# Relative-bias attention and a mixture of adapters: the bias row laid out anew, and the start-up order rewritten

## The chip, the cores and the metric

One core of a Trainium2 chip runs the whole kernel. The core has a matrix engine (PE in the profile; its weight loads are PEld), a vector engine (DVE), a scalar engine for activations (ACT), a general-purpose vector engine (GpSimd, POOL in the profile) and SyncE (SP), which here only issues transfers. Transfers are also issued from ACT and from POOL; all run on the core's 16 DMA engines. The metric is the device time of one execution, in microseconds (us).

## The reference

Eight batches of attention, eight heads, 576 positions, 64 values a head, with a bias that depends on the distance of two positions alone (at most 32 buckets, the last for every distance from 128 on); after it, on the rows of all heads side by side, a mixture of eight rank-16 adapters with the two best taken.

```python
B, H, S, D = 8, 8, 576, 64
scores = scale * q @ k.T                        # scale = 1/8
scores = scores + bias_table[bucket].transpose(2, 0, 1)[None]   # bucket = f(|i - j|)
attn = exp(scores - max) / sum
attn_out = attn @ v
x = attn_out as [B*S, H*D]                      # 4608 x 512
logits = x @ w_gate                             # 512 x 8, the two largest are kept, softmax of the two
out = x + sum over the two e of w_e * (x @ A[e]) @ B[e]
```

## The kernel before

**Tiling.** The 576 positions of a batch are 512 and a tail of 64. The 512 are dealt to partitions so that position 4p + j is partition p of group j, and the keys are cut into groups g = 0 to 3 of 128. Two heads, hp and hp + 4, make a pair; a batch has four pairs, and 32 pairs run through the kernel. Each pair has five steps: for g = 0 to 3 the scores of 128 keys against 512 queries for both heads, and for g = 4 the tails of both heads (tail keys against all queries, and all keys against the tail queries). That makes 160 steps. A step is `qk` on PE into one of two score buffers in PSUM (lines 375 and 381), `expo` on ACT (line 396), which turns 128 x 1024 scores into the probabilities p, and, for g below 4, `band_of` on DVE, which multiplies p near the diagonal with a table M of exp(bias).

**The bias.** Since the last bucket holds from distance 128 on, it is subtracted from all, and what is left is zero outside a band. For each head a row of 512 values over the signed distance is built in SBUF (`gg`: the row itself and its exponential, eight heads in eight partitions), written to DRAM (`g_d`), and read back so that each partition holds the stretch of the row that its own position needs: `Mr` (128 x 8 x 384, the exponentials, for M), `MHr` and `Br` (the plain row for the tails). From these, `band_table(hp)` on DVE copies M for one pair (line 287, 768 elements with the direction reversed), and `tail_bias(n)` on POOL copies B4 (n = 0 from MHr, n = 2 from Br) and BT (n = 1 from MHr). A tail step needs both parts of B4: PE adds them to the scores with a product by the identity (line 381, `sc<-B,ident`). BT goes into the 64 x 64 corner, `tail_scores` (lines 355 to 360).

**Other work of a pair.** `cast_kq` casts its k and q from f32 to bf16 (DVE for the first three pairs, POOL afterwards; `pkq` in the start-up list), `transposes` turns them on PE (line 337) with one copy on DVE (`kqT`), `cast_v` casts v, `pv` multiplies probabilities and values on PE (line 426, five slices: 0 to 3 for the 512 queries, 4 for the tail queries), `recip` and `norm` divide on DVE (`rn` in the list). Per batch: `tail_transposes` (line 346, `tt` in the list), `tail_scores` (`ts`), and the mixture of an earlier batch, spread over the steps by `MIX`: logits, gate in four parts, `m_z` (line 563), `m_zT`, four output blocks, tail output.

**Order.** Nothing is scheduled automatically: each engine runs its instructions in the order in which they are recorded. A step n records `qk(n+1)`, `expo(n)`, loads, the entries of `OPS[n]`, and then the regular work. `START` changes the order of the first 15 steps: the groups 0 to 3 of pairs 0, 1 and 2 come first, and then their tail steps, `(0, 4), (1, 4), (2, 4)`, as steps 12, 13 and 14. Step 15 is the first of pair 3, step 20 the first of batch 1. `OPS` holds the start-up work of steps 0 to 18: `ckq` casts of pairs 1 and 2, `T` transposes, `M` band tables, `b` bands, `cv` casts of v, `pv` and `rn`. `SPQ`, `POOLQ` and `POOLQ2` are the first transfers of SP and POOL, in order (`kq` k and q of a pair, `v` v of batch 0 in four parts of four transfers, `tl` and `vt` tails, `M`, `MH`, `Br` the three reads of the row). A cast on POOL made with `behind_dve` waits for the DVE instruction recorded just before it. The tail transfers of batch 1 are issued on POOL at steps 12 and 13.

The lines to follow: 71 (table load), 210 to 236 (the row), 238 (its write), 249, 257 and 263 (its three reads), 287 (M), 292, 296, 298 (tails), 175 (tail loads), 185 (casts on POOL), 305 (zeroing of second buffers on POOL). DVE's instructions all carry line 126, a helper that remembers the last one.

Of the kernel before, what the change touches and what calls it, by code (L numbers as in the profile page):

```python
# [10 lines left out]
FP32 = mybir.dt.float32  # L11
BF16 = mybir.dt.bfloat16
# [15 lines left out]
def kernel(  # L28
# [40 lines left out]
    btT = cp.tile([H, NB], FP32, tag="btT")  # L69
    for e in range(2):  # L70
        (nc.gpsimd if e else nc.scalar).dma_start(
            out=btT.rearrange("(c e) b -> e c b", e=2)[e],
            in_=bias_table.rearrange("b (e c) -> e c b", e=2)[e])
    warm = cp.tile([128, 1], FP32, tag="warm")
    nc.vector.memset(warm, 0.0)
    fill = cp.tile([128, 512], BF16, tag="fill")
    nc.vector.memset(fill, 1.0)
# [4 lines left out]
    START = ((0, 0), (0, 1), (0, 2), (0, 3), (1, 0), (1, 1), (1, 2), (1, 3), (2, 0), (2, 1),  # L82
             (2, 2), (2, 3), (0, 4), (1, 4), (2, 4))
    SPQ = (('v', 0), ('v', 1), ('M', 0, 8), ('v', 2), ('v', 3), ('kq', 0, 3), ('kq', 1, 0),
           ('kq', 1, 1), ('kq', 1, 2), ('kq', 1, 3), ('v1', 0), ('v1', 1), ('v1', 2),
           ('v1', 3))
    POOLQ = (('tl', 0, 0), ('tl', 0, 1), ('tl', 1, 0), ('tl', 1, 1), ('MH', 0), ('MH', 1),
             ('Br', 0), ('Br', 1), ('Br', 2), ('Br', 3))
    POOLQ2 = (('vt', 0), ('vt', 1), ('B', 0), ('B', 1), ('B', 2))
    OPS = {0: (('ckq', 1), ('T', 1)),  # L90
           3: (('ckq', 2),),
           4: (('T', 2),),
           5: (('pkq', 3, 0),),
           6: (('tt', 0),),
           7: (('pkq', 3, 1),),
           8: (('M', 0),),
           9: (('b', 0, 0), ('b', 0, 1)),
           10: (('M', 1), ('b', 0, 2), ('b', 0, 3), ('ts', 0), ('pkq', 4, 0)),
           11: (('cv', 0), ('b', 1, 0), ('b', 1, 1)),
           12: (('M', 2), ('b', 1, 2), ('b', 1, 3), ('T', 3), ('pkq', 4, 1)),  # L100
           13: (('cv', 1), ('b', 2, 0), ('b', 2, 1), ('pv', 0, 0), ('pv', 0, 1), ('pv', 0, 2),
                ('rn', 0, 0)),
           14: (('b', 2, 2), ('b', 2, 3), ('pv', 0, 3), ('pv', 0, 4), ('rn', 0, 1)),
           15: (('cv', 2), ('M', 3), ('pv', 1, 0), ('pv', 1, 1), ('pv', 1, 2), ('rn', 1, 0)),
           16: (('pv', 1, 3), ('pv', 1, 4), ('rn', 1, 1)),
           17: (('pv', 2, 0), ('pv', 2, 1), ('pv', 2, 2), ('rn', 2, 0)),
           18: (('cv', 3), ('tt', 1), ('pv', 2, 3), ('pv', 2, 4), ('rn', 2, 1))}
    LAST = ((2, 'pv', 0), (2, 'pv', 1), (1, 'eh', 7), (1, 'pv', 2), (1, 'pv', 3))

    def keep_busy(n, cols=512):  # L110
        ps = acp.tile([128, 512], FP32, name="fl", tag="acc")
        for _ in range(n):
            nc.tensor.matmul(ps[:, :cols], lhsT=fill[:, 0:128], rhs=fill[:, :cols],
                             start=True, stop=True, skip_group_check=True)
# [85 lines left out]
    for t in tls[:1] + vts[:1]:  # L200
# [7 lines left out]
    gg = cp.tile([H, 2, 512], BF16, tag="gg")  # L208
    g_sb = gg[:, 0]
    nc.gpsimd.memset(g_sb, 0.0)  # L210
    bsub = cp.tile([H, NB], FP32, tag="bsub")
    nc.gpsimd.tensor_scalar(bsub, btT, btT[:, NB - 1:NB], 1.0 / scale,
                      op0=ALU.subtract, op1=ALU.mult)
# [9 lines left out]
    while runs[nsm][0] == nsm and runs[nsm][2] == nsm + 1:  # L223
        nsm += 1
    nc.gpsimd.tensor_copy(g_sb[:, C:C + nsm], bsub[:, :nsm])
    nc.gpsimd.tensor_copy(
        g_sb[:, C - nsm + 1:C],
        bass.AP(tensor=bsub.tensor, offset=bsub.offset + nsm - 1,
                ap=[bsub.ap[0], [-1, nsm - 1]]))
    for bv, lo, hi in runs[nsm:]:  # L230
        n = hi - lo
        dst = bass.AP(tensor=g_sb.tensor, offset=g_sb.offset + C - hi + 1,
                      ap=[g_sb.ap[0], [hi - 1 + lo, 2], [1, n]])
        (nc.scalar.copy if bv % 3 else nc.gpsimd.tensor_copy)(
            dst, bsub[:, bv:bv + 1].unsqueeze(2).to_broadcast((H, 2, n)))
    nc.scalar.activation(gg[:, 1], g_sb, ACT.Exp, scale=scale)
    g_d = nc.dram_tensor("g_d", (H, 2, 512), BF16, kind="Internal")
    nc.scalar.dma_start(out=g_d.ap(), in_=gg)
# [4 lines left out]
    Mr = cp.tile([128, H, MW], BF16, tag="Mr")  # L243
    MHr = cp.tile([128, HP, 192], BF16, tag="MHr")
    Br = cp.tile([128, H, 64], BF16, tag="Br")

    def load_bias(h0, h1):
        for j in range(4):
            nc.sync.dma_start(
                out=Mr[j * 32:(j + 1) * 32, h0:h1],  # L250
                in_=bass.AP(tensor=gt.tensor, offset=gt.offset + h0 * 1024 + 512 + j,
                            ap=[[4, 32], [1024, h1 - h0], [1, MW]]))
# [3 lines left out]
    def load_br(j, eng):  # L256
        eng.dma_start(
            out=Br[j * 32:(j + 1) * 32],
            in_=bass.AP(tensor=gt.tensor, offset=gt.offset + 64 + j,
                        ap=[[4, 32], [1024, H], [1, 64]]))  # L260

    def load_mh(e, eng):
        eng.dma_start(
            out=MHr[e * 64:(e + 1) * 64],
            in_=bass.AP(tensor=gt.tensor, offset=gt.offset + e * 1024 + 192,
                        ap=[[1, 64], [2048, HP], [1, 192]]))

    for f, *a in SPQ:
        {"v": lambda j: load_v(0, (j,)), "M": load_bias, "kq": load_kq,
         "v1": lambda j: load_v(1, (j,)), "Br": lambda j: load_br(j, nc.sync),  # L270
         "MH": lambda e: load_mh(e, nc.sync)}[f](*a)
    for f, *a in POOLQ:
        {"tl": lambda w, e: load_tail(0, w, e), "Br": lambda j: load_br(j, nc.gpsimd),
         "MH": lambda e: load_mh(e, nc.gpsimd)}[f](*a)
# [7 lines left out]
    def at(t, off, *dims):  # L282
        return bass.AP(tensor=t.tensor, offset=t.offset + off,
                       ap=[t.ap[0]] + [list(d) for d in dims])

    def band_table(hp):
        dve.tensor_copy(M[:, 2 * hp:2 * hp + 2],
                        at(Mr, 2 * hp * MW + MW - 1, (MW, 2), (-1, 4), (-4, 96)))

    def tail_bias(n):  # L290
        if n == 0:
            return nc.gpsimd.tensor_copy(
                B4[:, :, 0:128].rearrange("p c (j u) -> p c j u", j=4),
                at(MHr, 191, (192, HP), (-1, 4), (-4, 32)))
        if n == 1:
            return nc.gpsimd.tensor_copy(BT.rearrange("p c (e t) -> p c e t", e=2),
                                         at(MHr, 63, (192, HP), (0, 2), (-1, 64)))
        nc.gpsimd.tensor_copy(  # L298
            B4[:, :, 128:256].rearrange("p c (e t) -> p c e t", e=2),
            at(Br, 63, (128, HP), (64, 2), (-1, 64)))  # L300

    for f, *a in POOLQ2:
        {"vt": lambda e: load_tail(0, 2, e), "B": tail_bias, "cv": cast_v}[f](*a)
    for t in tls[1:] + vts[1:]:
        nc.gpsimd.memset(t, 0.0)
    v_ones(nc.gpsimd, vts[1])
    nc.gpsimd.memset(vns[1][:, :, :, D:D1], 1.0)
# [522 lines left out]
    def pool_kq(i, w):  # L830
# [5 lines left out]
        "w": keep_busy, "vt": load_tail, "B": tail_bias,  # L836
        "ckq": lambda i: (cast_kq(i, 0, dve), cast_kq(i, 1, dve)), "pkq": pool_kq}

    MIX = (4, 9, 17, 19, 19, 19, 20, 20, 22, 24, 25, 27, 30, 32, 39)
# [110 lines left out]
```

## Time and profile before

| | us |
|---|---|
| three runs | 203.14, 203.54, 206.69 |
| median | 203.54 |
| the profiled execution, its own time | 202.09 |
| its span from the first to the last record | 200.3 |

In the profile a group of instructions is one line: where it starts, how long it was busy, engine, line of the kernel, what it writes and reads, how many, and in brackets how long the engine had been idle before it and what released it. Steps can be counted off on ACT: every `p<-sc` is one step, the first at 7.58 us. Counted so, step 11 starts at 18.97 us, step 14 at 26.98, step 20 at 36.47 and step 39 at 55.75.

The four stretches that the text speaks of, from the table by stretches (busy us, and the granted PE clock):

| us | PE | DVE | ACT | POOL | PE clock |
|---|---|---|---|---|---|
| 0 to 20 | 11.46 | 8.63 | 15.15 | 12.01 | 1.00 |
| 20 to 36.5 | 12.37 | 14.27 | 7.99 | 12.38 | 0.79 |
| 57.2 to 186 | 124.66 | 114.97 | 116.91 | 59.54 | 1.00 |
| 186 to 200.3 | 8.60 | 6.88 | 5.66 | 0.00 | 0.98 |

### The profile page before, as it was taken

What the parts mean: (1) busy time and instruction counts of PE and PEld (TensorE: products, weight loads), DVE (VectorE), ACT (ScalarE), POOL (GpSimd) and SP (SyncE); (2) the same over time, 40 slices, a digit from 0 to 9 for tenths busy, and PEclk for the clock granted to TensorE, in tenths of its full rate; (3) what the DMA queues carried; (4) which work ended last, traced back from release to release, by engine and by line L of the source; (5) the groups of instructions that cost most, each with busy time, mean ns of one, the idle gap of its engine ahead of it and who ended that gap; (6) DMA issues with size and microseconds to landing.
All of it is one profiled execution on the core that took longest, in us unless ns stands there. A gap on an engine that the chain in (4) does not pass through costs nothing.

```text
span 200.3 us, 6922 instructions
## 1 busy us (share of the span) xinstructions
PE 176.4 (88%) x2754; PEld 118.5 (59%) x2754; DVE 164.0 (82%) x446; ACT 165.7 (83%) x198; POOL 101.0 (50%) x184
## 2 busy tenths in 40 slices
PE   1785299899999999999999999999999999999980
PEld 0342177576666667766676666666666677567730
DVE  4515599999997998889988997999879987998680
ACT  2899337899979989898979898998799898999550
POOL 4783976598755457264735383446544342411000
PEclk9999759999999999999999999999999999999999
DMA  6999999899999988999999999999999946822176
GB/s 176 246 177 162 271 317 161 131 336 159 143 240 253 155 211 171 319 223 122 221 305 313 173 196 195 363 168 182 173 297 294 225 111 183 108 110 106 56 250 221
DMA packets 87060, 41.18 MB, mean 206 GB/s; under 512 B 66284, under 2 KB 83852, under 8 KB 87028
## 3 DMA queue, kind: packets, MB, share of 16 engines
q1 hardware_dynamic: 68512, 38.15, 80.2%
q0 software_dynamic: 18144, 2.18, 19.1%
q8 instruction: 21, 0.34, 0.7%
q10 hardware_dynamic: 372, 0.41, 0.7%
q14 instruction: 11, 0.09, 0.2%
HBM read 29.97 MB, written 9.45 MB: 197 GB/s over the span
## 4 chain that ended last, share of the span: by engine, by line
PE 65%; ACT 13%; DMA 9%; POOL 5%; issue 4%; DVE 0%; DVEq 0%; ACTq 0%; POOLq 0%
PE pv L426 16%; PE sc L375 15%; ACT p L396 11%; PE sc L381 8%; PE kqps L337 7%; PE zp L563 4%; DMA Br<-g_d 3%; PE dl L584 3%; DMA tl<-in_q_dram 2%; PE tps L346 2%; DMA g_d<-gg 2%; DMA btT<-in_bias_table_dram 2%; PE lp L519 1%; PE ztps L576 1%; PE tsc L355 1%
## 5 line engine op out<-in xcount | busy, mean ns | idle before, releaser
L396 ACT ACTIVATE p<-sc 128x1024 bf16<-128x1024 f32 x160 | 152.5, 1028 | 15.6 <-PE sc L381 10.5
L126 DVE TENSOR_TENSOR p<-p,M 128x512 bf16<-128x512 bf16 (+1 forms) x128 | 62.4, 509 | 0.1
L375 PE MATMUL sc<-kqT 64*128 64x512 bf16 x256 | 51.6, 402 | 7.6 <-ACT p L396 6.7
L426 PE MATMUL pv<-vn,p 128*128 128x65 bf16 x1240 | 57.6, 196 | 0.0
L426 PEld LDWEIGHTS <-p 128*128 128x128 bf16 x1364 | 48.9, 100 | 14.1 <-issue 9.3
L185 POOL CAST kqn<-qf 128x512 bf16<-128x512 f32 x29 | 18.1, 624 | 40.0 <-DVE rc L126 35.0
L126 DVE TENSOR_TENSOR x<-pv,rc 128x384 bf16<-128x384 f32 x64 | 29.0, 453 | 1.2
L185 POOL CAST kqn<-kf 128x512 bf16<-128x512 f32 x29 | 18.2, 629 | 22.6 <-DVE zT L126 6.3
L126 DVE COPY kqT<-kqps 128x1024 bf16<-128x1024 bf16 x32 | 22.0, 687 | 9.1 <-PE kqps L337 8.4
L337 PE MATMUL kqps<-ident,kqn 128*128 128x128 bf16 x256 | 21.9, 231 | 7.1 <-DVE kqn L126 4.5
L375 PEld LDWEIGHTS <-kqT 64*128 64x128 bf16 x256 | 12.9, 94 | 25.1 <-issue 17.9
L426 PE MATMUL pv<-vt,p 128*128 128x130 bf16 x124 | 27.4, 221 | 0.0
L337 PEld LDWEIGHTS <-kqn 128*128 128x128 bf16 x256 | 15.5, 102 | 15.4 <-issue 5.9
L189 POOL CAST vn<-vf 128x512 bf16<-128x512 f32 x28 | 19.3, 691 | 5.7 <-DVE rc L126 4.4
L126 DVE RECIPROCAL rc<-pv 128x6 f32<-128x6 f32 x64 | 11.6, 181 | 8.0 <-PE pv L426 7.1
L126 DVE TENSOR_TENSOR o<-dl,x 128x512 f32<-128x512 f32 x25 | 17.0, 680 | 0.4 <-PE dl L782 0.4
L381 PEld LDWEIGHTS <-kqT 128*128 128x128 bf16 x128 | 10.0, 99 | 7.6 <-issue 2.5
L381 PE MATMUL sc<-kqT,tlT 128*128 128x512 bf16 x32 | 12.3, 386 | 1.1 <-ACT p L396 1.0
L381 PE MATMUL sc<-tlT,kqT 128*128 128x128 bf16 x128 | 12.6, 221 | 0.0
L381 PE MATMUL sc<-B,ident 128*128 128x128 bf16 x64 | 9.1, 222 | 2.2 <-POOL B L298 2.2
L175 POOL DMA_DIRECT2D vt<-in_v_dram x16 | 10.1, 636 | 0.9 <-PE sc L375 0.9
L175 POOL DMA_DIRECT2D tl<-in_k_dram x16 | 9.9, 621 | 0.0
(123 smaller groups left out, 190.4 us busy)
## 6 DMA issues: line engine op xcount, KB each, us to landing
vf<-in_v_dram SPq DMA_DIRECT2D x128, 64.0 KB, 3.6
kf<-in_k_dram SPq DMA_DIRECT2D x6, 1024.0 KB, 6.8
qf<-in_q_dram SPq DMA_DIRECT2D x6, 1024.0 KB, 9.9
out_dram<-o SPq DMA_DIRECT2D x12, 512.0 KB, 5.6
kf<-in_k_dram SPq DMA_DIRECT2D x8, 256.0 KB, 4.9
qf<-in_q_dram SPq DMA_DIRECT2D x8, 256.0 KB, 4.9
out_dram<-o SPq DMA_DIRECT2D x7, 256.0 KB, 2.6
out_dram<-ot SPq DMA_DIRECT2D x7, 128.0 KB, 7.1
```

What stands on the lines that cost most here:

```text
L126: self.last = f(*a, **kw)
L175: nc.gpsimd.dma_start(out=o, in_=sr[e])
L185: return (eng or nc.gpsimd).tensor_copy(o, s)
L189: return (eng or nc.gpsimd).tensor_copy(vns[b % 2][:, :, hp:H:HP, :D], vfs[b][:, :, hp:H:HP, :])
L337: nc.tensor.transpose(o, n[:, w, j], ident)
L346: nc.tensor.transpose(ps[:, w, c, :], tls[b % 2][:, w, c, :], ident)
L375: nc.tensor.matmul(sc[:, h * 512:(h + 1) * 512], lhsT=t[s, 0, g * 128:(g + 1) * 128], rhs=t[s, 1, :], start=True, stop=True)
L381: nc.tensor.matmul(o, lhsT=lhsT, rhs=rhs, start=start, stop=stop, skip_group_check=True)
L396: nc.scalar.activation(p, scs.pop(n), ACT.Exp, scale=scale)
L426: nc.tensor.matmul(o, lhsT=lhsT, rhs=rhs, start=start, stop=stop, skip_group_check=True)
L563: nc.tensor.matmul(zp[:, t - t0, :], lhsT=xT[:, 4 * t + c, :], rhs=Ab[:, c, :], start=(t == t0 and c == 0), stop=(c == 3), skip_group_chec ...
L584: nc.tensor.matmul(ps, lhsT=zT[:, t, :], rhs=Bb, start=True, stop=True)
```

## The change

The row has the heads innermost: `gg` is 33 partitions x 512 distances x 8 heads. Partitions 0 to 31 hold the same plain row, partition 32 its exponential; two of them, 0 and 32, are written to DRAM, as a `g_d` of 2 x 4096 values. The table is loaded in one transfer that repeats it over the 33 partitions instead of two that turn it; the preparation goes from POOL and ACT to DVE, ACT and POOL. `Mr` is read in one transfer of 128 runs of 6144 bytes (before: four, 1024 runs of 768 bytes, the same 768 KB), `MHr` in one of 128 runs of 3072 bytes (before: two, 512 runs of 384 bytes; the bytes double, 192 KB to 384 KB), `Br` in one of 128 runs of 1024 bytes (before: four, 1024 runs of 128 bytes, the same bytes). The copies from them now step over the heads: 64 bytes between neighbouring elements for M and the first copy of B4, 16 bytes for the other two (before 8 bytes and 2). Pair 3's k and q come before v, step `(0, 4)` is step 8, `OPS` is rewritten, the zeroing of second buffers on POOL stands between transfers, and five entries of `MIX` move. `fill` and `keep_busy` fall away; nothing had called the latter.

```diff
-    btT = cp.tile([H, NB], FP32, tag="btT")
-    for e in range(2):
-        (nc.gpsimd if e else nc.scalar).dma_start(
-            out=btT.rearrange("(c e) b -> e c b", e=2)[e],
-            in_=bias_table.rearrange("b (e c) -> e c b", e=2)[e])
+    bt = cp.tile([33, NB, H], FP32, tag="bt")
+    nc.scalar.dma_start(out=bt, in_=bass.AP(tensor=bias_table.tensor, offset=bias_table.offset,
+                                            ap=[[0, 33], [1, NB * H]]))
...
-    fill = cp.tile([128, 512], BF16, tag="fill")
-    nc.vector.memset(fill, 1.0)
...
-    START = ((0, 0), (0, 1), (0, 2), (0, 3), (1, 0), (1, 1), (1, 2), (1, 3), (2, 0), (2, 1),
-             (2, 2), (2, 3), (0, 4), (1, 4), (2, 4))
-    SPQ = (('v', 0), ('v', 1), ('M', 0, 8), ('v', 2), ('v', 3), ('kq', 0, 3), ('kq', 1, 0),
+    START = ((0, 0), (0, 1), (0, 2), (0, 3), (1, 0), (1, 1), (1, 2), (1, 3), (0, 4), (2, 0),
+             (2, 1), (2, 2), (2, 3), (1, 4), (2, 4))
+    SPQ = (('kq', 0, 3), ('v', 0), ('M',), ('v', 1), ('v', 2), ('v', 3), ('kq', 1, 0),
...
-    POOLQ = (('tl', 0, 0), ('tl', 0, 1), ('tl', 1, 0), ('tl', 1, 1), ('MH', 0), ('MH', 1),
-             ('Br', 0), ('Br', 1), ('Br', 2), ('Br', 3))
-    POOLQ2 = (('vt', 0), ('vt', 1), ('B', 0), ('B', 1), ('B', 2))
+    POOLQ = (('tl', 0, 0), ('tl', 0, 1), ('tl', 1, 0), ('tl', 1, 1), ('ms', 0), ('MH',),
+             ('Br',), ('vt', 0), ('vt', 1), ('ms', 1), ('ms', 2))
+    POOLQ2 = (('B', 0), ('B', 1), ('B', 2))
     OPS = {0: (('ckq', 1), ('T', 1)),
            3: (('ckq', 2),),
-           4: (('T', 2),),
-           5: (('pkq', 3, 0),),
-           6: (('tt', 0),),
-           7: (('pkq', 3, 1),),
-           8: (('M', 0),),
-           9: (('b', 0, 0), ('b', 0, 1)),
-           10: (('M', 1), ('b', 0, 2), ('b', 0, 3), ('ts', 0), ('pkq', 4, 0)),
-           11: (('cv', 0), ('b', 1, 0), ('b', 1, 1)),
-           12: (('M', 2), ('b', 1, 2), ('b', 1, 3), ('T', 3), ('pkq', 4, 1)),
-           13: (('cv', 1), ('b', 2, 0), ('b', 2, 1), ('pv', 0, 0), ('pv', 0, 1), ('pv', 0, 2),
-                ('rn', 0, 0)),
-           14: (('b', 2, 2), ('b', 2, 3), ('pv', 0, 3), ('pv', 0, 4), ('rn', 0, 1)),
-           15: (('cv', 2), ('M', 3), ('pv', 1, 0), ('pv', 1, 1), ('pv', 1, 2), ('rn', 1, 0)),
...
-           17: (('pv', 2, 0), ('pv', 2, 1), ('pv', 2, 2), ('rn', 2, 0)),
-           18: (('cv', 3), ('tt', 1), ('pv', 2, 3), ('pv', 2, 4), ('rn', 2, 1))}
+           4: (('T', 2), ('tt', 0)),
+           5: (('M', 0), ('pkq', 3, 0)),
+           6: (('b', 0, 0), ('b', 0, 1), ('pkq', 3, 1)),
+           7: (('ts', 0), ('b', 0, 2), ('b', 0, 3), ('M', 1)),
+           8: (('b', 1, 0), ('b', 1, 1), ('T', 3)),
+           9: (('b', 1, 2), ('M', 2)),
+           10: (('b', 1, 3), ('pkq', 4, 0)),
+           11: (('cv', 0), ('b', 2, 0)),
+           12: (('pkq', 4, 1), ('b', 2, 1), ('b', 2, 2)),
+           13: (('b', 2, 3), ('pv', 0, 0), ('pv', 0, 1), ('pv', 0, 2), ('rn', 0, 0),
+                ('cv', 1)),
+           14: (('pv', 0, 3), ('pv', 0, 4), ('rn', 0, 1), ('M', 3)),
+           15: (('cv', 2), ('pv', 1, 0), ('pv', 1, 1), ('pv', 1, 2), ('rn', 1, 0)),
...
+           17: (('cv', 3), ('pv', 2, 0), ('pv', 2, 1), ('pv', 2, 2), ('rn', 2, 0)),
+           18: (('tt', 1), ('pv', 2, 3), ('pv', 2, 4), ('rn', 2, 1))}
...
-    nc.gpsimd.memset(g_sb, 0.0)
-    nc.gpsimd.tensor_scalar(bsub, btT, btT[:, NB - 1:NB], 1.0 / scale,
-                      op0=ALU.subtract, op1=ALU.mult)
+    gg = ldp.tile([33, 512, H], BF16, name="gg", tag="vf")
+    far = bass.AP(tensor=gg.tensor, offset=gg.offset,
+                  ap=[[gg.ap[0][0], 32], [383 * H, 2], [1, 129 * H]])
+    nc.gpsimd.memset(far, 0.0)
+    dve.memset(bass.AP(tensor=gg.tensor, offset=gg[32:33].offset,
+                       ap=[[gg.ap[0][0], 1], [383 * H, 2], [1, 129 * H]]), 1.0)
+    dve.tensor_tensor(bd, bt, bt[:, NB - 1:NB, :].to_broadcast((33, NB, H)), op=ALU.subtract)
+    nc.scalar.activation(tb[32:33], bd[32:33], ACT.Exp)
+    dve.tensor_scalar(tb[0:32], bd[0:32], 1.0 / scale, None, op0=ALU.mult)
...
-    nc.gpsimd.tensor_copy(g_sb[:, C:C + nsm], bsub[:, :nsm])
+    dve.tensor_copy(gg[:, C:C + nsm], tb[:, :nsm])
...
-        (nc.scalar.copy if bv % 3 else nc.gpsimd.tensor_copy)(
+        (nc.scalar.copy if n > NSPLIT else nc.gpsimd.tensor_copy)(dst, src)
-    nc.scalar.activation(gg[:, 1], g_sb, ACT.Exp, scale=scale)
-    g_d = nc.dram_tensor("g_d", (H, 2, 512), BF16, kind="Internal")
-    nc.scalar.dma_start(out=g_d.ap(), in_=gg)
+    G = 512 * H
+    g_d = nc.dram_tensor("g_d", (2, 4, G // 4), BF16, kind="Internal")
+    nc.scalar.dma_start(out=g_d.ap(), in_=bass.AP(
+        tensor=gg.tensor, offset=gg.offset,
+        ap=[[gg.ap[0][0] * 32, 2], [G // 4, 4], [1, G // 4]]))
...
-    def load_bias(h0, h1):
-        for j in range(4):
-            nc.sync.dma_start(
-                out=Mr[j * 32:(j + 1) * 32, h0:h1],
-                in_=bass.AP(tensor=gt.tensor, offset=gt.offset + h0 * 1024 + 512 + j,
-                            ap=[[4, 32], [1024, h1 - h0], [1, MW]]))
+    def load_bias(eng=nc.sync):
+        eng.dma_start(
+            out=Mr.rearrange("p x h -> p (x h)"),
+            in_=bass.AP(tensor=gt.tensor, offset=gt.offset + G,
+                        ap=[[H, 4], [4 * H, 32], [1, MW * H]]))
...
-                        at(Mr, 2 * hp * MW + MW - 1, (MW, 2), (-1, 4), (-4, 96)))
+                        at(Mr, (MW - 1) * H + hp, (HP, 2), (-H, 4), (-4 * H, 96)))
...
-                at(MHr, 191, (192, HP), (-1, 4), (-4, 32)))
+                at(MHr, 191 * H, (1, HP), (-H, 4), (-4 * H, 32)))
...
-    MIX = (4, 9, 17, 19, 19, 19, 20, 20, 22, 24, 25, 27, 30, 32, 39)
+    MIX = (4, 10, 17, 19, 19, 20, 20, 22, 22, 24, 25, 27, 27, 32, 39)
```

On the engines this leaves, in order. DVE: `warm`, zeroing of the tail buffers, the ones in partition 32 (2 x 1032 values), the subtraction, the scaling, two copies into the row, and only then the first cast of k. ACT: the exponential of one partition (256 values), five copies of 160 to 256 values, the write of the row, step 0. POOL: zeros in 32 partitions, nine copies of 48 to 128 values, the four tail loads, the zeroing of `tl1`, `MHr`, `Br`, two v tails, the other zeroing, the three tail copies, and then the casts of pair 3.

## The prediction

> **What bounds the kernel now.** First the page's busy times and slices, to find the stretch that is not full.
>
> ```profile
> PE 176.4 (88%) x2754; PEld 118.5 (59%) x2754; DVE 164.0 (82%) x446; ACT 165.7 (83%) x198; POOL 101.0 (50%) x184
> ...
> PE   1785299899999999999999999999999999999980
> ...
> DVE  4515599999997998889988997999879987998680
> ACT  2899337899979989898979898998799898999550
> ...
> PEclk9999759999999999999999999999999999999999
> ```
>
> A slice is 5 us. From 40 us on PE, DVE and ACT are all near full. The hole is from 20 to 35 us: ACT 3, 3, 7 tenths, PE 2 in the first slice with its clock down to 7 and 5 tenths. Second, ACT's timeline around it, where steps can be counted:
>
> ```profile
> 18.48 0.60 ACT L360 ACTIVATE ptl<-tsc 128x512 bf16<-128x512 f32 x1
> 18.97 1.02 ACT L396 ACTIVATE p<-sc 128x1024 bf16<-128x1024 f32 x1
> 21.52 1.94 ACT L396 ACTIVATE p<-sc 128x1024 bf16<-128x1024 f32 x2 [1.53 <-PE sc L381]
> 26.98 1.02 ACT L396 ACTIVATE p<-sc 128x1024 bf16<-128x1024 f32 x1 [3.52 <-PE sc L381]
> 29.38 1.94 ACT L396 ACTIVATE p<-sc 128x1024 bf16<-128x1024 f32 x2 [1.37 <-PE pv L426]
> ```
>
> Steps 12 and 14 wait 1.53 and 3.52 us for tail scores. Third, the chain of waits from 7 to 37 us, which says why:
>
> ```profile
> 7.21 3.42 DMA g_d<-gg
> 10.63 0.28 issue
> 10.92 1.25 POOL MHr L263 x2
> ...
> 13.88 6.20 DMA Br<-g_d
> ...
> 20.29 0.92 POOL B L298
> 21.21 0.89 POOL tl L305
> ...
> 28.71 1.80 POOL tl L175 x3
> 30.50 4.51 DMA tl<-in_q_dram
> ```
>
> The row's way through DRAM, then POOL's copies and zeroing, then pair 3's casts, then the tail loads of batch 1, which land at 35.0 and let step 20 start at 36.47. Fourth, DVE in the timeline, the other engine that has no slack there:
>
> ```profile
> 17.91 0.56 DVE L126 COPY M<-Mr 128x768 bf16<-128x768 bf16 x1 [2.26 <-DMA Mr<-g_d]
> ...
> 22.80 0.43 DVE L126 CAST vn<-vf 128x512 bf16<-128x512 f32 x1 [2.06 <-DMA vf<-in_v_dram]
> ```
>
> It waits for Mr and for v and is then busy without a gap to 36 us. From step 20 to 39 the kernel needs 19.28 us (55.75 - 36.47), 1.01 a step against ACT's 0.95 back to back (4.79 / 5), so a gain is the amount by which step 20 comes earlier, plus what `MIX` brings.
>
> **Part 1, first step.** DVE loses `fill` (0.48) but gets, in front of the first cast, ones into 2064 values: `fill` wrote 512 in 0.48, so 1.94. Then subtraction 0.36 (nearest: `x<-pv,rc` 192 values, 0.36), scaling 0.2, a wait for ACT's exponential, two copies of 128 values at 0.2. From the end of `vn` at 2.23 (2.77 less 0.54): ones to 4.2, both copies to about 5.5, two casts of 0.43 to 6.3. Today the second cast ends at 5.02. Step 0 moves from 7.58 to 8.9, +1.3. Bounds: +0.3 if the ones cost as `tl` does (1024 bf16 values in 0.48 as words), +2 if POOL's copies hold DVE up. The table's landing is not the limit: POOL's came 3.39 us after issue, so about 4.1 for a transfer issued at 0.74, just before the ones end.
>
> **Part 2, the row.** ACT: 0.2 + five copies of some 0.3 (6 to 28 values took 0.11 each, 512 took 0.60) = 1.7. POOL: nine of some 0.24 (0.19 for 16, 0.61 for 512) = 2.2, beside ACT. From 5.0 the row is ready at 7.2, as now (7.21); bounds 6.3 and 8.5. Its write took 3.42 from eight partitions; I take 3.4, bounds 2.5 and 5. The Trainium skill speaks against two partitions: DMA: Bandwidth & Descriptors, "Why a DMA increments its semaphore by 16 and not by 1", says that the engines used are the largest number up to 16 that divides the slowest dimension of both sides, so 2 in place of 8. By it each would carry 8 KB in place of 2, an estimate of some tenths more and inside the bounds; no row here shows it.
>
> **Part 3, the reads.** Mr: one issue (0.45) in place of four (1.80). Bytes from g_d are now 768 + 384 + 128 KB = 1.31 MB. In 24 to 28 us, where 1 KB runs were read, the DMA engines moved 348 GB/s, in 15 to 18 us, with runs of 128 to 768 bytes, 178. At 348 the three need 3.8 us, so Mr is there at about 15.2 (10.7 + 4.5), against 17.9. Bounds 13.7, and 18 if one 8 KB place in DRAM does not serve faster. POOL issues MHr and Br in 2 x 0.63 in place of 6 (3.6 us), to 12.0; landed by 16.0 (MHr's 4.7 today); copies 0.64 + 0.61 + 0.92, so B4 is complete at 18.2, against 21.21.
>
> **Part 4, wider steps in the copies.** For M the trace has no such reading; the 8-byte step costs nothing (0.56, as the band product of 768 values with 0.55). Lower bound 0; upper the longest M row, 1.77, which lies beside POOL's casts. I take +0.15, since the step known to be free is the nearest. POOL's three copies I leave at 2.17 (an 8-byte step took 0.64, a 2-byte one 0.61), bounds 1.8 without the stretch to 0.92, and 3 x 1.77. The skill speaks against this too: GPSIMD Engine Reference, "7. Performance pitfalls for Q7 kernels", gives half as much again for steps above 8 bytes. By it the three copies would take 3.3 us in place of 2.2, and B4 would be complete at 19.3.
>
> **Part 5, step 8 is now a tail step.** By ACT's pace it would start at 8.9 + 8 x 0.95 = 16.5; it gets B4 at 18.2, so at 18.6: 2 us lost, where today 1.53 is lost at step 12. What queues behind it on PE: `tail_scores`, step 9, transposes of pair 3. PE's pause is then under 3 us, today it is idle from 19 to 24 but for B's 0.73. By ACT alone step 20 follows at 18.6 + 12 x 0.95 + 0.5 (`ptl`) = 30.5.
>
> **Part 6, POOL behind it.** The zeroing (0.95 + 0.52 + 0.47 + small, 21.16 to 23.36 today) now lies where POOL waits for MHr; it costs nothing if that wait is real (12.0 + 1.3 for two v tails + 1.1 is before 16). Pair 3's casts start at 18.2 in place of 23.36 and end, with a v tail between them (0.65 + 0.62 + 0.63), at 20.1; kqT is on DVE to 21.4. Pair 4's casts need its k, which SP issues behind twelve v transfers at 0.69: 11.2 + 8.3 = 19.5. The first loads landed 2.7 and 3.3 after issue, the median is 4.9; with 4.0, k is there at 23.5 and q at 24.0, both cast by 24.8, the fourth tail load issued at 26.7 (three issues of 0.62 ahead of it) and landed 4.5 later, at 31.2 against 35.0. Step 20 came 1.4 after that: 32.6, with 4.9 for the landing 33.5. kq(0,3) ahead of v costs SP two issues, 0.95, that it has spare before the row lands.
>
> **Part 7, DVE.** From Mr at 15.2: M 0.7, four bands 1.92, M, two bands, 19.5; kqT until 21.4; band, M, band, 23.1; v landed by then (19.0 + 4); then the cast of v (0.42), four bands (1.92), three times rn (1.28), three more casts (1.26), M (0.7), kqT, tlT (0.69 each), two bands (0.96): 10.5, so 33.6, and step 20 comes 0.7 before the end of these as it does today (36.47 against 37.15): 32.9. Today 3.2 us of bands and copies come after 22.80 that now come before it.
>
> **Part 8, `MIX`, six batches.** `m_z` leaves the step in which ACT waits 0.8 a batch for `tsc`. PE's idle time is 0.8 and 0.6 in 21.3 and 21.65 us, so at most 3 x 0.8 + 3 x 0.6 = 4.2 in all; two outputs fall in one step (one more DVE 0.68), at worst 4.1 the other way. The bulk of PE's work is untouched: I take a seventh, -0.6.
>
> **Sum.** Parts 5, 6 and 7 give 30.5, 32.6 and 32.9 for step 20; I take 32.6, the landing's middle value, near which the third comes too. Against 36.47 that is -3.9, and -0.6 for `MIX`: -4.5. The profiled execution took 202.09 (span 200.3), so 197.6 of that kind. It lies 1.4 below the median of the runs shown, 203.54, and I keep the difference: 199.0.
>
> **The rivals.** *Only ACT bounds it*: if the row's reads land a microsecond or two sooner and v comes early, parts 6 and 7 follow ACT's 30.5, and `MIX` gives 1.5: -6.0 - 1.5 = -7.5, 196.0. For it: ACT has no other wait; against: DVE's list is as long as before. *The transfers decide*: 1.31 MB are read from one small place, and kq and v stand behind them; if Mr lands at 18 as now, DVE starts as today, keeps the 2.06 wait for v, and the tail loads of batch 1 come at 34: -1 to -2, 202. For it: SP's v transfers wait for others to land already. *Slower*: the copies with 64-byte steps. M stands four times in DVE's full stretch and the tails' copies three times in a row on POOL in front of pair 3's casts, which DVE then waits for. If each takes the longest M row and the step's own 0.15 (1.92, +1.36 over 0.56), that is 7 x 1.36 = 9.5 on one chain, less 4.5: +5.0, 208.5; from +1.23 each on it passes 2%. For it: the 0.92 and 1.77 rows show that such copies can stretch; against: both have the other engine of the two beside them.
>
> **How the numbers follow.** Forecast 0.50 (its own range 197 to 201), ACT alone 0.24, transfers 0.16, slower 0.10. About 2% is what a measurement of this kernel can tell from no change, that is 199.5 and 207.6. The forecast lies below 199.5 in two of three (0.33), and ACT alone wholly: faster 0.57. Within 2%: 0.17 + 0.16 = 0.33. Slower 0.10. The range takes the forecast, most of the second and of the third: 195.6 to 202.8.
>
> **What would show it.** Right: M's first copy near 15 with no v wait of 2 us after it, B4 complete near 18, one ACT wait of about 2 us at step 8 and none above 1 us after it, granted clock 1.00 from 20 to 30 us, tail loads of batch 1 landed at 31, step 20 at 32 to 33. Wrong: step 0 later than 10, M's copies above 0.9, Mr landing at 17 or later, or a stretch of 57 to 186 us that changes by more than 1.5 us.

## The result, and the profile after

| us | before | after |
|---|---|---|
| median of four runs | 203.57 (203.14 to 206.69) | 219.62 (217.92 to 220.97) |
| the profiled execution, its span | 202.09, 200.3 | 220.97, 219.2 |

The changed kernel is slower: the ratio of its runs to those of before is 1.079 (95% interval 1.069 to 1.090). 199.0 was predicted, with a range of 195.6 to 202.8. The starts of the steps on ACT say when the time is lost:

| start of step (us) | 0 | 5 | 8 | 12 | 20 | 39 | 99 | 159 |
|---|---|---|---|---|---|---|---|---|
| before | 7.58 | 12.12 | 15.50 | 21.52 | 36.47 | 55.75 | 120.00 | 184.35 |
| after | 9.11 | 14.10 | 37.60 | 41.22 | 52.22 | 71.51 | 135.50 | 203.06 |

Step 20 comes 15.75 us later, and the medians differ by 16.05: the loss is made before step 20, by one wait between steps 7 and 8. (The wait is longer than the loss: from step 8 to step 20 after takes 14.62 us and before 20.97, since before has waits of its own there.) From step 99 to 159 this execution took 3.2 us more than before's; e1 and e15 below, the second with before's row, order and `MIX`, took 2.6 and 2.1 more there, so this isn't peculiar to the change.

The page of after, its 40 slices of 5.5 us (rows as before; the last two are the DMA engines' busy share in tenths and what they moved):

```profile
PE   0582004899999999999999999999998979999990
...
DVE  6740070979899789979998999799988975899680
ACT  3573002978999998998998989899988877899660
...
DMA  6979236997999996979998999699999999652166
GB/s 176 268 98 82 97 81 166 292 147 155 327 145 98 280 223 119 205 172 349 176 183 180 366 161 189 133 318 203 164 219 295 276 198 187 78 170 99 43 215 224
```

From 22 to 33 us PE and ACT stand still, and this time so do the DMA engines: 2 and 3 tenths, under 100 GB/s. A kernel that waits for transfers while the engines that carry them are mostly idle may be waiting for transfers that use few of them; the experiments test this. ACT's timeline has the hole in one row, POOL's and DVE's say for what:

```profile
16.37 1.94 ACT L400 ACTIVATE p<-sc 128x1024 bf16<-128x1024 f32 x2 [1.23 <-PE sc L379]
37.11 0.60 ACT L364 ACTIVATE ptl<-tsc 128x512 bf16<-128x512 f32 x1 [18.80 <-PE sc L385]
37.60 4.68 ACT L400 ACTIVATE p<-sc 128x1024 bf16<-128x1024 f32 x5
...
11.66 1.09 POOL L261 DMA_DIRECT2D MHr<-g_d  x1
...
32.77 1.04 POOL L300 COPY B<-MHr 128x512 bf16<-128x512 bf16 x1 [16.88 <-DMA MHr<-g_d]
33.76 1.10 POOL L304 COPY BT<-MHr 128x512 bf16<-128x512 bf16 x1
34.80 1.09 POOL L306 COPY B<-Br 128x512 bf16<-128x512 bf16 x1
...
28.58 0.81 DVE L116 COPY M<-Mr 128x768 bf16<-128x768 bf16 x1 [12.06 <-DMA Mr<-g_d]
```

ACT waits 18.8 us for `ptl`, which PE can make only behind step 8's product with B4, which POOL copies from MHr, issued at 11.66 and there at 32.7. Mr, issued at 11.01, lets M be copied at 28.58. The chain of waits has the same in one piece (start, duration, what):

```profile
8.08 2.70 POOL tl L165 x4
10.78 0.88 POOL tl L272
11.66 21.07 DMA MHr<-g_d
...
34.80 1.11 POOL B L306
35.95 1.13 PE sc L385
```

By stretches (PE, PEld, DVE, ACT, POOL busy us, PE clock, DMA share, GB/s):

```profile
22.00:28.00 6.00, 0.00 (x0) 0.00 (x0) 0.00 (x0) 0.00 (x0) 0.00 (x0) 1.00 0.30 94
```

All five engines idle for 6 us, and the DMA share is 0.30 (four engines of 16, always busy, would be 0.25).

### The profile page after: what moved, and what is told of

Its sections match the earlier page's. It is cut to its first block, busy times and chain, and to the rows that moved or that the text cites. A ratio compares the mean times of both kernels' runs of the same rounds, so it can differ in the third digit from the quotient of the medians.

```text
span 219.2 us, 6906 instructions
## 1 busy us (share of the span) xinstructions
PE 175.9 (80%) x2738; PEld 120.8 (55%) x2754; DVE 167.6 (76%) x450; ACT 166.3 (76%) x193; POOL 101.6 (46%) x181
## 4 chain that ended last, share of the span: by engine, by line
PE 52%; DMA 22%; ACT 11%; POOL 4%; issue 4%; DVE 3%; SPq 0%; DVEq 0%; ACTq 0%; POOLq 0%
PE pv L430 15%; PE sc L379 12%; DMA xT<-x 11%; ACT p L400 10%; DMA MHr<-g_d 10%; PE sc L385 8%; PE kqps L341 5%; PE zp L567 3%; PE lp L523 2%; DMA vf<-in_v_dram 2%; DVE kqT L116 1%; PE dl L588 1%; POOL tl L165 1%; PE tps L350 1%; POOL gg L232 1%
## 5 line engine op out<-in xcount | busy, mean ns | idle before, releaser
L379 PE MATMUL sc<-kqT 64*128 64x512 bf16 x256 | 52.3, 409 | 9.3 <-ACT p L400 6.8
L116 DVE COPY kqT<-kqps 128x1024 bf16<-128x1024 bf16 x32 | 22.1, 690 | 15.7 <-PE kqps L341 15.2
L175 POOL CAST kqn<-qf 128x512 bf16<-128x512 f32 x29 | 18.2, 627 | 32.4 <-DVE rc L116 28.5
L379 PEld LDWEIGHTS <-kqT 64*128 64x128 bf16 x256 | 13.4, 94 | 25.2 <-issue 17.1
L341 PEld LDWEIGHTS <-kqn 128*128 128x128 bf16 x256 | 16.0, 104 | 15.0 <-DVE kqn L116 7.8
L179 POOL CAST vn<-vf 128x512 bf16<-128x512 f32 x28 | 18.4, 657 | 10.5 <-DMA vf<-in_v_dram 5.8
L364 ACT ACTIVATE ptl<-tsc 128x512 bf16<-128x512 f32 x8 | 4.8, 597 | 21.0 <-PE sc L385 18.8
L116 DVE TENSOR_TENSOR o<-dl,x 128x512 f32<-128x512 f32 x25 | 16.5, 680 | 0.4 <-PE dl L786 0.4
L385 PEld LDWEIGHTS <-ident 128*128 128x128 bf16 x64 | 5.2, 102 | 15.6 <-issue 15.6
L385 PE MATMUL sc<-kqT,tlT 128*128 128x512 bf16 x32 | 12.8, 399 | 1.3 <-ACT p L400 1.3
L385 PE MATMUL sc<-tlT,kqT 128*128 128x128 bf16 x128 | 13.1, 227 | 0.0
```

The lines of the kernel that those rows point to most:

```text
L116: self.last = f(*a, **kw)
L175: return (eng or nc.gpsimd).tensor_copy(o, s)
L179: return (eng or nc.gpsimd).tensor_copy(vns[b % 2][:, :, hp:H:HP, :D], vfs[b][:, :, hp:H:HP, :])
L341: nc.tensor.transpose(o, n[:, w, j], ident)
L364: nc.scalar.activation(p, ps, ACT.Exp, scale=scale)
L379: nc.tensor.matmul(sc[:, h * 512:(h + 1) * 512], lhsT=t[s, 0, g * 128:(g + 1) * 128], rhs=t[s, 1, :], start=True, stop=True)
```

## The experiments

The main theory, F: a transfer is spread over no more DMA engines than divide the slowest dimension on both of its sides. The row's new reads have 4 there (Mr and Br) and 2 (MHr), those of before had 32 and 64. Its rival P: the place or the runs, 768 KB from 8 KB of DRAM in runs of 6144 bytes. After that the question was why the change gains nothing even when F is undone.

**e1**: after, with the reads in the old number of transfers, by partitions.

```diff
-        eng.dma_start(out=Mr.rearrange("p x h -> p (x h)"),
-            in_=bass.AP(..., offset=gt.offset + G, ap=[[H, 4], [4 * H, 32], [1, MW * H]]))
+        for j in range(4):
+            eng.dma_start(out=Mr[j * 32:(j + 1) * 32].rearrange("p x h -> p (x h)"),
+                in_=bass.AP(..., offset=gt.offset + G + j * H, ap=[[4 * H, 32], [1, MW * H]]))
```

(MHr in two of 64 partitions and Br in four of 32 in the same way.)

> All three reads of the row split into transfers whose slowest dimension is 32 or 64 on both sides (Mr 4 x 32 partitions, MHr 2 x 64, Br 4 x 32); layout, run lengths, bytes and order stay. Theory F (few engines: a transfer is spread only over as many DMA engines as divide the slowest dimension of both sides, so 4 for Mr and Br, 2 for MHr): M's first copy at 15 to 17 us in place of 28.6, B4 complete at 18 to 20 in place of 35.9, step 20 at 32 to 35, time 200 to 204. Theory P (one place: long runs from one 8 KB place in DRAM are served slowly, however many engines ask): M's first copy at 25 or later, time 215 or more.

**e2** splits Mr alone, **e3** MHr and Br alone.

> Only Mr is split into 4 x 32 partitions; MHr and Br stay one transfer each. Theory F: Mr lands by 15 to 17, MHr on its two engines still needs most of its 21 us, so step 8 starts at 30 or later and the time is 212 to 218. Theory P: both land as now, 219.

> Only MHr (2 x 64) and Br (4 x 32) are split; Mr stays one transfer. Theory F: B4 is complete at 18 to 21 and step 8 starts by 21, M's first copy stays at 24 to 29 and DVE is late by some 10 us, time 208 to 216. Theory P: both land as now, 219.

**e4**: the kernel before, its old layout and its runs of 768 bytes, but Mr in one transfer a head, whose slowest dimension is 4.

```diff
-        for j in range(4):
-            nc.sync.dma_start(out=Mr[j * 32:(j + 1) * 32, h0:h1], in_=...ap=[[4, 32], [1024, h1 - h0], [1, MW]])
+        for h in range(h0, h1):
+            nc.sync.dma_start(out=Mr[:, h], in_=...ap=[[1, 4], [4, 32], [1, MW]])
```

> The kernel before, with Mr read in eight transfers, one for each head, whose source has 4 as its slowest dimension, in place of four of 32 partitions; bytes and run length (768 bytes) stay, so neither the new layout nor long runs are in it. Theory F: Mr lands 8 us or more later (M's first copy at 26 or later in place of 17.9) and the time is 210 to 217. Theory P: M's first copy within 2 us of 17.9, time 203 to 206.

**e8**: e3 with Mr in two transfers, each with a slowest dimension of 2.

> e3_split_tails with Mr read in two transfers of 64 partitions whose source has 2 as its slowest dimension, in place of one with 4. Theory F: both run on the same two engines, Mr needs about twice its 17 us, M's first copy at 40 to 47, time 222 to 235. Theory P: two transfers in place of one change nothing, M's first copy at 27 to 30.

Measured, against runs of before on the same chip (one run each for e2, e3, e4, e8; e2 to e4 on e1's chip):

| us | time | M's first copy | B4 complete | step 8 | step 20 |
|---|---|---|---|---|---|
| before | 203.57 | 17.91 | 21.21 | 15.50 | 36.47 |
| after | 219.62 | 28.58 | 35.9 | 37.60 | 52.22 |
| e1 (205.47 before) | 207.05, ratio 1.0095 (1.0014 to 1.0177) | 19.48 | 22.6 | 24.27 | 39.16 |
| e2 | 211.77 | 21.78 | 29.9 | 31.63 | 46.50 |
| e3 | 213.73 | 28.57 | 25.5 | 27.23 | 46.74 |
| e4 | 209.35 | 18.13 | 20.6 | 15.80 | 43.97 |
| e8 (205.46 before) | 219.82 | 35.69 | 24.2 | 25.90 | 54.08 |

F holds: e1's ratio is 1.0095 where after's is 1.079, e2 and e3 take back a part each, and each cures the transfer that it splits. e8 slows Mr further, in the same place and with the same runs, and e4 slows the old kernel with its short runs. P can explain neither. Nor is it the number of transfers: e4 has eight in place of four and e8 two in place of one, and both are slower. The share of the DMA engines shows their number, here e8 while Mr is all that moves:

```profile
21.00:24.00 3.00, 0.27 (x1) 0.10 (x1) 0.00 (x0) 0.00 (x0) 2.15 (x3) 1.00 0.13 39
```

0.13 is two of 16. Sizes went wrong. In e1 to e3 what was cured came 2.5 to 4.8 us after its expected range (M at 19.48 and 21.78 for 15 to 17, B4 at 22.6 for 18 to 20 and at 25.5 for 18 to 21). e8's M was expected at 40 to 47, since half the engines should take twice as long, and came at 35.69. e4's was expected at 26, though its first copy needs two heads only and so came at 18.13, the wait falling later (step 14 at 33.89), and its time, 209.35, lies just under the range. The trace also records each DMA packet, with its size and time. Of the row's reads, "us an engine" being the packets' times divided by the engines used (most often two of Mr's packets are under way at once in e8, four in after and 16 in e1):

```
             Mr: packets, median ns, us an engine, first to last   MHr: us an engine    Br: us an engine
before       1024 x  768 B   59   3.9 on 16   11.7 to 16.9          0.9 on 16            0.6 on 16
e1            128 x 6144 B  447   3.3 on 16   12.5 to 18.3          1.9 on 16            0.6 on 16
e9            128 x 6144 B  362   3.0 on 16   11.8 to 17.7          1.6 on 16            0.5 on 16
after         128 x 6144 B  351  12.4 on  4   12.4 to 27.4
e8            128 x 6144 B  247  19.4 on  2   12.7 to 35.0
```

e8's miss is in it: 19.4 us an engine, and not twice 12.4. A packet's time depends on what else is under way. On e8's two engines it was 411 to 448 ns in the mean from 12 to 18 us, beside other transfers, and a median of 247 from 24 to 30, with a DMA share of 0.14 to 0.27; on after's four, 412 to 606 from 14 to 20 us and a median of 235 to 260 from 20 to 28, with a share of 0.25 to 0.38. So fewer engines aren't slower ones each; Mr in e8 moved in quieter company for longer. Long runs are worth 0.6 us of Mr (3.9 to 3.3); MHr, which now reads twice the bytes, costs 1.0 more. In sum 5.4 before and 5.8 in e1: spread as before, the new layout reads no faster.

**What is left: e5 to e7.** e5 is the kernel before with the new START, SPQ, POOLQ, OPS and MIX alone; e6 is the new row (with e1's reads) in the old order; e7 is e1 with the three `tail_bias` copies on ACT (`nc.scalar.copy`, between steps 6 and 7), so that they stand in nobody's way on POOL.

> The row as before (heads in partitions, short runs, its ten reads), but START, SPQ, POOLQ, OPS and MIX of the changed kernel. Theory L (the layout is what loses once the reads are spread: POOL's and DVE's copies with wide steps, and the two hindering each other): B4 complete by 20, four bands after M in 2.2 us, step 8 at 20 to 21, step 20 at 33 to 35, time 1 to 4 us below the kernel before. Theory S (the order loses: the tail step in eighth place stops ACT too early): 1 to 4 us above the kernel before.

> The new row with its reads split as in e1_split, but START, SPQ, POOLQ, OPS and MIX of the kernel before. Theory L: B4 complete at 22.5 or later, step 12 there or later, time 2 to 5 us above the kernel before. Theory S: within 1.5 us of the kernel before.

> e1_split with the three tail copies on ACT, between steps 6 and 7, in place of POOL. Theory L: the copies take 0.6 to 0.7 each there, the four bands beside them take 2.2 us or less in place of 4.5, step 8 starts at 20 to 22 in place of 24.3, time 2 to 4 us below e1_split. If POOL's copies and their hold on DVE are not what costs, the time stays within 1 us of e1_split.

Measured: e5 1.0039 (0.9983 to 1.0094), step 20 at 39.14; e6 1.0049 (0.9990 to 1.0109), 38.38; e7 1.0085 (1.0038 to 1.0132), 40.12. Neither half gains by itself, and neither theory is borne out: L wanted e5 shorter by 1 to 4 us and e6 longer by 2 to 5 (it is 1.0 longer), and the 1 to 4 us that S wanted e5 longer aren't clear of noise either (its interval reaches from 0.3 us shorter to 1.9 longer). The starts of step 20 are to be read with care: the profiled execution of before, 202.09, is shorter than every timed run of before (202.18 to 211.16), so its step 20 at 36.47 is an early one. The ratios are the comparison. In e1, DVE's and POOL's timelines show what the new steps cost there:

```profile
19.48 0.86 DVE L116 COPY M<-Mr 128x768 bf16<-128x768 bf16 x1 [2.96 <-DMA Mr<-g_d]
20.45 4.49 DVE L116 TENSOR_TENSOR p<-p,M 128x512 bf16<-128x512 bf16 x4
...
18.52 1.03 POOL L303 COPY B<-MHr 128x512 bf16<-128x512 bf16 x1 [1.12 <-DMA MHr<-g_d]
19.49 1.83 POOL L307 COPY BT<-MHr 128x512 bf16<-128x512 bf16 x1
21.37 1.20 POOL L309 COPY B<-Br 128x512 bf16<-128x512 bf16 x1
```

POOL's copies take 4.1 us where before took 2.2, and four bands beside them 4.49, where e5, with POOL idle beside them, took 1.70. But e7 takes the copies away from POOL, the bands take 2.52 (now beside POOL's casts of pair 3), step 8 starts at 25.22, and nothing is won. On ACT's timeline of e7 one sees why:

```profile
19.08 1.07 ACT L303 COPY B<-MHr 128x512 bf16<-128x512 bf16 x1 [1.75 <-DMA MHr<-g_d]
21.75 1.12 ACT L309 COPY B<-Br 128x512 bf16<-128x512 bf16 x1 [1.61 <-DMA Br<-g_d]
22.78 1.14 ACT L307 COPY BT<-MHr 128x512 bf16<-128x512 bf16 x1
25.22 4.68 ACT L403 ACTIVATE p<-sc 128x1024 bf16<-128x1024 f32 x5
```

Br lands at 21.7, so B4 is complete no sooner than in e1. (The copies took 1.07 to 1.14 on ACT where 0.6 to 0.7 was expected, perhaps for the wide steps; no run has them on ACT with narrow ones.)

**e9**: does the one small place limit the reads once 16 engines carry them? e1, with Mr's 768 KB from k.

> The kernel of e1, but the four transfers of Mr (the same 768 KB in the same rows of 6144 bytes) read from 768 KB of k in place of the row's 8 KB. They still start only when the row has landed. M is so made of other values: the band's bias is left out. What it asks: with 16 engines at work, is the one 8 KB place in DRAM what holds Mr to 7.9 us from issue to M's first copy (e1: 11.5 to 19.5)? If the place limits: Mr is there within 5 us of its issue, M's first copy starts at 15.5 to 17, the DMA engines move 300 GB/s or more from 13 to 18 us, and step 8 still waits for Br and MHr. If the place does not matter, and Mr only shares full engines with kq(0,3) and v: first copy at 18.8 to 20.5, 200 to 230 GB/s as in e1, total 205 to 208.

Measured: 205.69, one run; M's first copy at 18.46, 7.8 us after issue (e1: 7.9), 219 GB/s from 13 to 18 us in both. Mr's packets take 3.0 us in sum in place of 3.3, and that is all: the place isn't the limit.

**e10**: e5 with the tail steps back in places 12 to 14. **e11**: before, with the zeroing on POOL moved, and MIX.

> The kernel of e5 (row and reads of before, order of after) with one thing put back: the tail steps (0,4), (1,4), (2,4) are steps 12, 13 and 14 again, tail_scores stands at step 10 and the transposes of pair 3 at step 12. If the tail step in eighth place is what takes the gain of the order: ACT has no wait above 2 us before step 12, step 12 starts within 0.5 us of B4's completion (22 to 23), step 20 at 35.5 to 37.5, time 1.5 to 3 us below e5, a ratio of 0.988 to 0.998. If it is pair 3's loads ahead of the row, or the bands' places, step 20 stays at 38.5 to 39.5 and the ratio at 1.000 to 1.008.

> The kernel before with two parts of the change alone: POOL's zeroing of the second batch's tiles moved to where POOL waits for MHr, and the new MIX. Row, reads, START, SPQ and OPS are those of before. If POOL's list decides when step 20 starts (the chain of before: POOL's B, zeroing, casts of pair 3, tail loads): casts of pair 3 start at 21.2 to 21.7 in place of 23.36, the tail loads of batch 1 land at 33 to 33.5, step 20 starts at 34.5 to 35.3, and with 0.35 from MIX the time is 1.5 to 2.3 us below before, a ratio of 0.988 to 0.993. If DVE's list from the landing of v (22.8) on decides: step 20 stays at 36 to 36.5 and the ratio is 0.997 to 1.000, MIX alone.

e10: 1.0031 (0.9986 to 1.0076). The wait of 7.3 us that e5's ACT has before step 8 is gone and step 12 starts at 22.81, 0.35 after B4; but step 20 starts at 38.52, which is the expectation's second case: the tail step's place isn't what takes the gain. e10's trace shows what step 20 waits for:

```profile
26.48 0.62 POOL L185 CAST kqn<-kf 128x512 bf16<-128x512 f32 x1 [1.54 <-DMA kf<-in_k_dram]
28.64 0.74 POOL L185 CAST kqn<-qf 128x512 bf16<-128x512 f32 x1 [1.54 <-DVE kqT L126]
29.33 1.36 POOL L175 DMA_DIRECT2D tl<-in_k_dram  x2
...
36.90 0.38 PE L353 MATMUL tps<-ident,tl 128*128 128x128 bf16 x4 [0.55 <-DMA tl<-in_q_dram]
...
38.52 1.94 ACT L403 ACTIVATE p<-sc 128x1024 bf16<-128x1024 f32 x2 [3.01 <-PE sc L382]
```

PE gets the tails of batch 1 at 36.9. POOL issues them behind the casts of pair 4, of which the first waits for its k and the second for DVE. SP issues that k at 22.11 (before: 19.84), since twelve transfers of v stand between Mr and it, where before had eight and pair 3's two. In e5, with the tail step eighth, another engine is full on the way to step 20, by the stretches again:

```profile
28.00:39.10 11.10, 11.08 (x187) 8.58 (x186) 8.79 (x23) 7.92 (x8) 6.20 (x10) 0.81 1.26 208
```

PE has no pause from 28 us to step 20 (10.81 of the same 11.10 us in e1): what it could not do while ACT waited at step 8 stands in front. These two are read from the traces; no run put pair 4's k earlier or took work from PE there.

e11: 0.9921 (0.9870 to 0.9972), the only kernel that came out shorter, yet its step 20 starts at 37.17, where 34.5 to 35.3 was expected, so not for the reason expected. Its two parts by themselves, **e14** (MIX) and **e15** (zeroing):

> The kernel before with the new MIX alone. e11 was shorter than before by 0.8% (0.9921, interval 0.987 to 0.9972), but its profile showed neither an earlier step 20 (37.17) nor a shorter stretch from step 39 to 159 (128.63 against 128.60). If MIX is what e11 gained by: ratio 0.990 to 0.995, steps 39 to 159 in 127.0 to 128.0 us. If MIX is worth the 0.35 us seen in the profile of e2 (128.25) or nothing: ratio 0.997 to 1.001.

> The kernel before with POOL's zeroing alone moved to where it waits for MHr. If the zeroing is what e11 gained by: ratio 0.990 to 0.995 and step 20 before 36. If not, since the casts of pair 3 then wait for their k (24.15 in e11 against 23.36 in before): ratio 0.998 to 1.002, step 20 at 36.3 to 37.3.

1.001 (0.9962 to 1.0058) and 1.0035 (0.9994 to 1.0076): neither gains by itself. So e11's 0.8% stays open: it may be scatter, or something that the two do only together. For the zeroing POOL's timeline of e15 shows the reason:

```profile
20.37 0.69 POOL L309 COPY B<-Br 128x512 bf16<-128x512 bf16 x1 [2.13 <-DMA Br<-g_d]
23.52 0.63 POOL L185 CAST kqn<-kf 128x512 bf16<-128x512 f32 x1 [2.46 <-DMA kf<-in_k_dram]
```

Two us of zeroing are gone from between these rows, and a wait for pair 3's k of 2.46 us is in their place. Before, the cast started at 23.36, its k having landed at 23.24.

**e12 and e13**: do v's runs of 256 bytes fill the DMA engines? e1 and the kernel before, with the first batch's v in runs of 1024.

> The kernel of e1 (the change with its reads spread over 16 engines), with the first batch's v read in runs of 1024 bytes in place of 256: the same 16 transfers of 64 KB into the same places, but each partition gets four rows of two heads, not one row of eight. Left out: the right order of v in the first batch. What it asks: from 8 to 22 us every kernel here has full DMA engines (share 1.2) that move only 166 to 180 GB/s, where from 22 to 28 us, with runs of 1024 bytes, before moved 347. If v's short runs fill the engines and so hide what the row's reads could gain: 8 to 22 us moves 230 GB/s or more, M's first copy is at 15.5 to 17.5 in place of 19.5, B4 complete at 19.5 to 21, step 8 at 20 to 22, step 20 at 34 to 36.5, time 3 to 5 us below e1's 1.0095, a ratio of 0.985 to 0.995. If not: 180 GB/s, M at 19 to 20, step 20 at 38.5 to 39.5, ratio 1.005 to 1.012.

> The kernel before with the same edit of v alone. If v's short runs fill the engines: 230 GB/s or more from 8 to 22 us in place of 166, M's first copy at 15 to 16.5, no wait of DVE for v above 1 us, the tail loads of batch 1 issued from 25 to 27 in place of 28.7, step 20 at 32.5 to 35, ratio 0.980 to 0.990. If the row's own layout were what kept the kernel before back, e12 would be at least 1 us shorter than this one; if the row's layout is worth nothing even then, e12 is the same or longer. If v's runs play no part: step 20 at 36 to 37 and a ratio of 0.998 to 1.003.

Measured: e12 1.0077 (1.0028 to 1.0126), M's first copy at 19.26, step 20 at 39.32; e13 1.0033 (0.9969 to 1.0098), 19.43 and 37.68. The packets from 8 to 22 us fall from 6582 (before) to 4044 (e13) and the DMA share from 1.27 to 1.06, but the rate stays, 166 and 158 GB/s, and neither kernel is shorter: v's runs aren't the bound, and the row's layout is worth nothing without them either. (e13's step 0 started at 10.12 where before's did at 7.58; why isn't known. From the landing of the row's write to M's first copy it took 7.2 us, before 7.3.)

## Why the prediction was wrong

**The step that failed is Part 3**: "At 348 the three need 3.8 us, so Mr is there at about 15.2". It gave the new reads the rate of other transfers, which run on 16 engines, and took "one issue (0.45) in place of four (1.80)" for a saving. The four transfers were what gave Mr a slowest dimension of 32. Part 2 quotes the very rule, of the Trainium skill, DMA: Bandwidth & Descriptors, "Why a DMA increments its semaphore by 16 and not by 1", for the row's write, where little hung on it, and Part 3 doesn't ask it of the reads, whose `ap=[[H, 4], ...]` and `ap=[[HP, 2], ...]` stand in the diff. It says that the number of engines, k, is the largest up to 16 that divides both slowest dimensions: 4 and 2 here. This case agrees: Mr's packets took 12.4 us on each of four engines against 3.3 on 16, and M's first copy came at 28.58. The second fault in the same step is the rate itself, which counts the three reads alone: from 8 to 22 us before's DMA engines had a share of 1.27 at 166 GB/s, with v's and the tails' packets among the row's, and in such company Mr's packets took 414 ns in the mean (e1) where 247 were enough in quiet (e8). So even spread, Mr lets M start at 19.5 (e1), not 15.2, and a rival that Part 3 names as its bound, "18 if one 8 KB place in DRAM does not serve faster", was nearer, though not for the place (e9).

**Parts 5 to 7 stand on it.** Part 5 has step 8 at 18.6, with B4 at 18.2: measured 37.60, and 24.27 in e1. That step 8 follows B4 held, but by 1.7 us in both, not by the 0.4 taken: `tail_scores` and ACT's `ptl`, recorded in step 7, stand between. Its weak point is one it didn't price: once the tail step comes eighth, ACT has nothing to do until B4 is there, and each us of B4's lateness is a us of ACT's. But e10 shows that this alone isn't what eats the gain. Part 6 has the tail loads of batch 1 issued by 26.7; no kernel here started its first before 28.7 (before 28.71, e10 29.33, e15 28.82, e1 31.82). It says that the zeroing moved aside lets pair 3's casts start at once. With the change's order of transfers they do (e10: B4 complete at 22.46, the cast at 22.41); in before's order, e15, they wait for their k instead and start at 23.52 in place of 23.36. The chain of waits of before showed POOL's zeroing, and hid the transfer that was about as late. But Part 6 had SP issue pair 4's k at 19.5 and both casts done by 24.8; in e10 these are 22.11 and 29.38. Part 7's sum for DVE was 32.9; in e1 the copy of the tails that step 20 needs comes at 38.42, after bands that took 4.49 in place of the 1.92 taken. And no part has a sum for PE from step 12 on, which had almost no pause from step 12 to step 20, 10.78 us of 11.00, in after. What would give these starts a gain, with the old row, no run shows: not the zeroing (e15), not the tail step's place (e10), not v's runs (e13).

In sum, step 20 came 19.6 us after the forecast's 32.6: 17.7 lie in B4 (35.9 for 18.2), 1.3 between B4 and step 8, and 0.6 between step 8 and step 20 (14.6 for 14.0). That the last stretch came out so near is partly luck, since its sum left out the engine that filled it.

**What was right, and nearly.** Part 1: step 0 at 8.9, measured 9.11; the ones took 1.78 (1.94 taken). Part 2: the write was issued at 8.49, at its upper bound of 8.5, because POOL's copies, ten and not nine, took 2.60 (2.2 taken); it landed 2.5 later (3.4 taken). Part 4: M's copy takes 0.81, where 0.71 was taken. POOL's three copies were left at 2.17; the rule quoted beside that, of the Trainium skill, GPSIMD Engine Reference, "7. Performance pitfalls for Q7 kernels" (half as much again for steps above 8 bytes), gave 3.3, and e3, where DVE stands idle beside them, measured 1.03 + 1.10 + 1.10 = 3.23. The rule had the direction and the choice had not; that its sum fits is partly luck, since 2.17 holds a copy stretched to 0.92. In e13 the three narrow ones took 0.64 + 0.61 + 0.61 = 1.86, and 3.23 is three quarters more than that. Part 8's 0.6 for `MIX` isn't shown: steps 39 to 159 took 128.60 before, and with the new `MIX` 128.25 in e2, 128.50 in e8 and 128.63 in e11, so it gives 0 to 0.35, and e14 can't tell it from nothing.

**The rivals.** The slower one, with 0.10, had the sign and another cause: copies with wide steps at 1.92 each. They cost 0.25 more for M (0.81 against 0.56) and 0.2 to 0.5 more each on POOL (1.03, 1.10 and 1.10 against 0.64, 0.61 and 0.92). "The transfers decide" had the resource and not the size: it let Mr land as late as before, and no rival let a transfer become slower than it was.

## What to carry to other kernels

When several transfers are joined into one, write down the slowest dimension of both sides before and after: a dimension of 4 put in front, to save three issues of 0.45 us, let M start 10.7 us later. Split such a load by partitions so that 16 divides the first dimension, as it does the 32 and 64 of e1. And when a stall is to be removed, look for the transfer that ends just behind it: the zeroing on the critical chain was worth nothing in that order of transfers, because what the next instruction reads landed no earlier than the zeroing ended.

## What the runs showed of the hardware

The number of DMA engines that a transfer used went with its slowest dimension: most often two packets of Mr were under way at once with 2 (e8), four with 4 (after) and 16 with 32 (e1). A packet's time went with what else the engines carried: 6144 bytes took 247 ns on two engines in quiet and 235 to 260 (medians) on four, but 411 ns and more on the same engines beside other transfers, and 414 in the mean on 16 in e1. In such company size mattered little: 768 bytes took 59 ns in before (13.0 bytes a ns), 6144 took 447 in e1 (13.7); the same 768 bytes took 36 ns in e4, where Mr's packets ran later and on four engines. One thing that shares the engines then and wasn't tried: in before POOL's queue took 38.8% of the 16 engines' time from 8 to 22 us for 0.53 MB, the tail loads' packets of 128 bytes at 32 ns each among them. (Shares above 1 say that packets of one engine overlap, so a packet's time isn't what it costs the engine.)

DVE's bands stretch beside POOL's work, with wide steps or without: four of them took 4.49 us in e1, beside POOL's copies and a cast, 2.52 in e7, beside its casts alone, and 1.70 in after and in e5, where POOL stood still.
